# Loading the first x rows as four tiles instead of two halves, with per-tile transposes and a shorter warm-up, in a fused MLP forward and backward kernel

## The chip, the cores and the metric

The kernel runs on one core of one Trainium2 chip. The metric is device time in microseconds (us). All comparisons below are between runs in the fast state (the state in which nearly all executions agree); one profile that fell in a slow state is named where it occurs and is not used, and of two kernels that were run once only (e14 and e15), whose state cannot be judged, the profile is read and no time is compared. "Span" is the length of one execution in its trace; it is mostly about 1.8 us shorter than the reported time of the same run.

## The reference

`x` is 2048 x 640, `w1` 640 x 1536, `w2` 1536 x 640, all bfloat16. The reference computes the output and the three gradients.

```
h   = x @ w1
a   = silu(h)
out = a @ w2
# and, by jax.vjp with grad_out: grad x, grad w1, grad w2
```

## The kernel before

All x rows are worked on in four chunks of 512 rows. Every matmul of the first stage (`h = x @ w1`) needs x transposed, with the 640 columns on the partitions in five slices (`DT` = 5). For chunks 1 to 3 a DMA transpose does that. For the first chunk the kernel wants to begin early, so it loads plain x rows, transposes them on the tensor engine (PE), and copies the result from PSUM to `xT`. Some instructions, collected in `early`, are moved ahead of the barrier that every engine passes at entry.

```python
NWARM = 22                     # dummy matmuls that keep PE busy while data arrives
KM = 2                         # the first two slices of w1 come first
warm = cpool.tile([P, P], dt_in, name="warm")
early = [nc.vector.memset(warm[:], 1.0)]
for i in range(NWARM):
    early.append(nc.tensor.matmul(wp[:, 0:P], lhsT=warm[:], rhs=warm[:], start=True, stop=True))
# ... cut ...
def load_x_half(half):         # 256 rows, two neighbouring rows on each partition: 2,560 B runs
    lo = half * 2 * P
    return nc.sync.dma_start(
        out=x_two[:, half, :, :], in_=x2[lo:lo + 2 * P, :].rearrange("(p q) d -> p q d", q=2)
    )

def load_w1_rows(lo, hi):      # row blocks of w1, first 512 columns
    return nc.sync.dma_start(out=w1_nat[:, lo:hi, 0:FC], in_=w1_v[:, lo:hi, 0:FC])

early += [load_x_half(0), load_x_half(1), load_w1_rows(0, 1), load_w1_rows(1, KM)]
load_w1_rows(KM, DT)
start_before_entry_wait(nc, {i.ins.name for i in early})
for fc in range(1, NFC):
    load_w1(fc * FC, (fc + 1) * FC)
# ... cut ...
def pe_x_half(xT, half):
    lo = half * 2 * P
    for dt_ in range(DT):
        tp = ps_h.tile([P, 2, P], dt_in, name="tp", tag="hp")
        for q in range(2):
            nc.tensor.transpose(tp[:, q, :], x_two[:, half, q, dt_ * P:(dt_ + 1) * P], ident[:])
        copy = nc.scalar.copy if dt_ % 2 else nc.vector.tensor_copy
        copy(out=xT[:, dt_, lo:lo + 2 * P].rearrange("p (s q) -> p q s", q=2), in_=tp[:])
```

The first stage then starts with slices 0 and 1 of four output blocks (eight matmuls of 512 columns), and only the ninth matmul needs slices 2 to 4:

```python
def h_first(xT, aT, ghT):
    # ...
    for dt_ in range(KM):                    # eight matmuls: w1 row blocks 0 and 1
        for ft in range(FB):
            h_mm(hps[ft], ft, xT, dt_, dt_ + 1)
    for i in range(FT + LAG_G):
        if i < FT:
            if i < FB:
                h_mm(hps[i], i, xT, KM, DT)  # the ninth matmul and on: w1 row blocks 2 to 4
    # ... cut ...
```

Below, the first, second and third w1 load are `load_w1_rows(0, 1)`, `load_w1_rows(1, KM)` and `load_w1_rows(KM, DT)`, which bring row block 0, row block 1 and row blocks 2 to 4 (384 KB). They are the same loads in both kernels.

Of the kernel before, what the change touches and what calls it, by code (L numbers as in the profile page):

```python
# [42 lines left out]
def kernel(  # L43
# [11 lines left out]
    nc = tc.nc  # L55
    P = 128
    x2 = x.flatten_outer_dims()
# [5 lines left out]
    S, D = x2.shape  # L63
    F = w1.shape[1]
    ST, DT, FT = S // P, D // P, F // P
    SC = 512
    NCH = S // SC
    STC = SC // P
# [3 lines left out]
    LAG = 2  # L72
    LAG_G = 4
    KM = 2
    NWARM = 22
    dt_in = x.dtype

    dram = ctx.enter_context(tc.tile_pool(name="dram", bufs=1, space=bass.MemoryType.DRAM))
# [2 lines left out]
    ps_h = ctx.enter_context(tc.tile_pool(name="ps_h", bufs=8, space=bass.MemoryType.PSUM))  # L81
# [8 lines left out]
    x_nat = natpool.tile([P, ST, D], dt_in, name="x_nat")  # L90
# [3 lines left out]
    x_v = x2.rearrange("(st p) d -> p st d", p=P)  # L94
# [4 lines left out]
    def store_rows(c, pool):  # L99
        for scr, dst_v in ((oT_scr, out_v), (gxT_scr, gx_v)):  # L100
            o_sb = pool.tile([P, STC, D], dt_in, name="o_sb")
            nc.sync.dma_start_transpose(out=o_sb[:], in_=scr[:, c * SC:(c + 1) * SC])
            nc.sync.dma_start(out=dst_v[:, c * STC:(c + 1) * STC, :], in_=o_sb[:])
# [8 lines left out]
    with ExitStack() as mctx:  # L112
        cpool = mctx.enter_context(tc.tile_pool(name="cpool", bufs=1))
# [7 lines left out]
        early = [nc.vector.memset(warm[:], 1.0)]  # L121
        warm_a = cpool.tile([P, 1], FP32, name="warm_a")
        wp = ps_h.tile([P, SC], FP32, name="wp", tag="hp")
        for i in range(NWARM):
            early.append(nc.tensor.matmul(wp[:, 0:P], lhsT=warm[:], rhs=warm[:], start=True, stop=True))

        ident = cpool.tile([P, P], dt_in, name="ident")
# [7 lines left out]
        def load_xT(c):  # L135
            xT = xpool.tile([P, DT, SC], dt_in, name="xT")
            nc.sync.dma_start_transpose(out=xT[:], in_=x2[c * SC:(c + 1) * SC, :])
            return xT

        def load_goT(c):  # L140
            goT = xpool.tile([P, DT, SC], dt_in, name="goT")
            nc.sync.dma_start_transpose(out=goT[:], in_=go2[c * SC:(c + 1) * SC, :])
            return goT

        xT_next = xpool.tile([P, DT, SC], dt_in, name="xT")
        x_two = cpool.tile([P, 2, 2, D], dt_in, name="x_two")

        def load_w1(lo, hi):
            nc.sync.dma_start(out=w1_nat[:, :, lo:hi], in_=w1_v[:, :, lo:hi])

        def load_x_half(half):
            lo = half * 2 * P
            return nc.sync.dma_start(
                out=x_two[:, half, :, :], in_=x2[lo:lo + 2 * P, :].rearrange("(p q) d -> p q d", q=2)
            )

        def load_w1_rows(lo, hi):
            return nc.sync.dma_start(out=w1_nat[:, lo:hi, 0:FC], in_=w1_v[:, lo:hi, 0:FC])

        early += [load_x_half(0), load_x_half(1), load_w1_rows(0, 1), load_w1_rows(1, KM)]  # L160
        load_w1_rows(KM, DT)
        start_before_entry_wait(nc, {i.ins.name for i in early})
        for fc in range(1, NFC):
# [5 lines left out]
            nc.sync.dma_start_transpose(out=w2T[:, :, fc * FC:(fc + 1) * FC], in_=w2[fc * FC:(fc + 1) * FC, :])  # L169
        nc.sync.dma_start_transpose(out=w1T[:], in_=w1[:, :])  # L170

        def pe_x_half(xT, half):
            lo = half * 2 * P
            for dt_ in range(DT):
                tp = ps_h.tile([P, 2, P], dt_in, name="tp", tag="hp")
                for q in range(2):
                    nc.tensor.transpose(tp[:, q, :], x_two[:, half, q, dt_ * P:(dt_ + 1) * P], ident[:])  # L177
                copy = nc.scalar.copy if dt_ % 2 else nc.vector.tensor_copy
                copy(out=xT[:, dt_, lo:lo + 2 * P].rearrange("p (s q) -> p q s", q=2), in_=tp[:])  # L179

        pe_x_half(xT_next, 0)
        pe_x_half(xT_next, 1)

        def h_mm(hp, ft, xT, lo, hi):
            for dt_ in range(lo, hi):
# [20 lines left out]
        def h_group(ft, xT, aT, ghT):  # L206
            hp = ps_h.tile([P, SC], FP32, name="hp")
            h_mm(hp, ft, xT, 0, DT)
            silu_a(ft, hp, aT)
            silu_grad(ft, hp, aT, ghT)  # L210

        def h_first(xT, aT, ghT):
            hps = []
            for ft in range(FB):
                hps.append(ps_h.tile([P, SC], FP32, name="hp"))
            for dt_ in range(KM):
# [5 lines that stand above are left out]
                        h_mm(hps[i], i, xT, KM, DT)  # L222
                    else:
                        hps.append(ps_h.tile([P, SC], FP32, name="hp"))
                        h_mm(hps[i], i, xT, 0, DT)
                    silu_a(i, hps[i], aT)
                if i >= LAG_G:
                    silu_grad(i - LAG_G, hps[i - LAG_G], aT, ghT)

        def g_group(ft, goT, ghT):  # L230
            gp = ps_h.tile([P, SC], FP32, name="hp")
            for dt_ in range(DT):
                nc.tensor.matmul(  # L233
                    gp[:],
                    lhsT=w2T[:, dt_, ft * P:(ft + 1) * P],
                    rhs=goT[:, dt_, :],
                    start=(dt_ == 0),
                    stop=(dt_ == DT - 1),
                )
            nc.vector.scalar_tensor_tensor(  # L240
                out=ghT[:, ft, :], in0=ghT[:, ft, :], scalar=1.0, in1=gp[:], op0=ALU.add, op1=ALU.mult
            )

        def sd_phase(c, w_all, rhs_all, scr):
            oT = opool.tile([P, DT, SC], dt_in, name="oT")
            for dt_ in range(DT):
                op_ = ps_h.tile([P, SC], FP32, name="hp")
                for ft in range(FT):
                    nc.tensor.matmul(  # L249
                        op_[:],  # L250
                        lhsT=w_all[:, ft, dt_ * P:(dt_ + 1) * P],
                        rhs=rhs_all[:, ft, :],
                        start=(ft == 0),
                        stop=(ft == FT - 1),
                    )
                if dt_ % 2 == 0:
                    nc.scalar.activation(oT[:, dt_, :], op_[:], ACT.Copy)  # L257
                else:
                    nc.vector.tensor_copy(out=oT[:, dt_, :], in_=op_[:])  # L259
            nc.sync.dma_start(  # L260
                out=scr[:, c * SC:(c + 1) * SC].rearrange("(dt p) s -> p dt s", p=P), in_=oT[:]
            )

        for c in range(NCH):
            xT, goT = xT_next, goT_next
            aT = apool.tile([P, FT, SC], dt_in, name="aT")
            ghT = apool.tile([P, FT, SC], dt_in, name="ghT")

            if c + 1 < NCH:
                xT_next = load_xT(c + 1)  # L270
                goT_next = load_goT(c + 1)
            if c == 1:
                for j in range(0, ST, STC):
                    nc.sync.dma_start(out=go_nat[:, j:j + STC, :], in_=go_v[:, j:j + STC, :])
            if c == 2:
                for j in range(0, ST, STC):
                    nc.sync.dma_start(out=x_nat[:, j:j + STC, :], in_=x_v[:, j:j + STC, :])

            if c == 0:
                h_first(xT, aT, ghT)  # L280
                nc.sync.dma_start(
                    out=aT_scr[:, c * SC:(c + 1) * SC].rearrange("(ft p) s -> p ft s", p=P), in_=aT[:]
                )
                sd_phase(c, w2_nat, aT, oT_scr)
                for ft in range(FT):
                    g_group(ft, goT, ghT)
                nc.sync.dma_start(
                    out=ghT_scr[:, c * SC:(c + 1) * SC].rearrange("(ft p) s -> p ft s", p=P), in_=ghT[:]
                )
                sd_phase(c, w1T, ghT, gxT_scr)  # L290
                continue

            for i in range(FT + LAG):
                if i < FT:
                    h_group(i, xT, aT, ghT)
                if i >= LAG:
                    g_group(i - LAG, goT, ghT)

            store_rows(c - 1, opool)
            nc.sync.dma_start(  # L300
                out=aT_scr[:, c * SC:(c + 1) * SC].rearrange("(ft p) s -> p ft s", p=P), in_=aT[:]
            )
            nc.sync.dma_start(
                out=ghT_scr[:, c * SC:(c + 1) * SC].rearrange("(ft p) s -> p ft s", p=P), in_=ghT[:]
            )
            if c == NCH - 1:
                load_a_blk(0, w1pool, "w1a")

            sd_phase(c, w2_nat, aT, oT_scr)
            sd_phase(c, w1T, ghT, gxT_scr)  # L310

    with ExitStack() as fctx:
# [45 lines left out]
        for fc in range(NFC):  # L358
            gh_blk = gh_blks[fc]
            for dt_ in range(DT):  # L360
                if dt_ == DT // 2:
                    store_gw2(fc)
                if fc == NFC - 1 and dt_ == DT - 1:
                    for k, (lo, hi) in enumerate(((0, FC - P), (FC - P, FC))):
# [12 lines left out]
                        else:  # L377
                            nc.vector.tensor_copy(out=g1[:, lo:hi], in_=gp[:, lo:hi])  # L378
                        nc.sync.dma_start(
                            out=gw1_v[:, dt_, fc * FC + lo:fc * FC + hi], in_=g1[:, lo:hi]  # L380
# [48 lines left out]
```

## Time and profile before

| | before |
|---|---|
| median of the first three runs | 321.46 us (320.92 to 321.84) |
| span of the profiled run | 318.9 us |
| PE busy | 315.2 us, 99% of the span |
| first real matmul starts | 5.01 us |

The first fence is the head of the page, then the share of the chain of waits by engine. Columns of the first line: busy time, share of the span, number of instructions.

```profile
PE 315.2 (99%) x1498; PEld 145.4 (46%) x1498; DVE 102.2 (32%) x182; ACT 77.7 (24%) x142; POOL 0.7 (0%) x6
...
PE 98%; DMA 1%; DVE 1%; issue 0%; DVEq 0%; SPq 0%
...
L186 PE MATMUL hp<-xT,w_nat 128*128 128x512 bf16 x240 | 56.9, 379 | 0.2 <-DVE xT L179 0.2
```

PE is the bound. The `| 0.2` in the last line is all the idle time just before first-stage matmuls. So, apart from a tail of 2.9 us after the last matmul, only the head, before the first real matmul, can shrink. The next fence is the chain of waits of the kernel before in its first 22 us; columns are start, duration and what the chain went through.

```profile
0.09 2.94 DMA x_two<-in_x_dram
...
3.08 0.41 PE tp L177 x2
3.49 0.02 issue
3.51 1.46 DVE xT L179 x4
4.97 0.04 issue
5.01 13.11 PE hp L186 x60
```

Read it from top to bottom: the first half of x lands, two transposes, four VectorE copies back to back, then 60 matmuls without a gap. The timeline of PE alone in the first 12 us of the kernel before (start, duration, count, and in brackets what ended the idle time before) shows warm-up, transposes and first stage:

```profile
0.50 2.53 PE L125 MATMUL wp<-warm 128*128 128x128 bf16 x22 [0.50 <-DVE warm L121]
3.08 1.70 PE L177 MATMUL tp<-ident,x_two 128*128 128x128 bf16 x20
5.01 7.28 PE L186 MATMUL hp<-xT,w_nat 128*128 128x512 bf16 x33 [0.23 <-DVE xT L179]
```

The pitch, start to start, tells the clock. The start times in the trace give 0.107 us for a 128-column matmul up to about 3.6 us and 0.056 us after; from 5.01 us a 512-column matmul starts every 0.216 us. So the array went from half to full speed near 3.6 us. Finally, the landing times of w1's three row-block loads (issue to completion, minimum, median, maximum), and the traffic between 3.5 and 5.5 us, where the last two columns are the share of the 16 DMA engines in use and GB/s:

```profile
DMA to landing us min/median/max: 3.3/3.7/4.2
```

```profile
core 0: us, PE busy (x) PEld busy (x) DVE busy (x) ACT busy (x) POOL busy (x), PEclk, DMA share, GB/s
3.50:5.50 2.00, 1.76 (x21) 1.23 (x20) 1.99 (x6) 1.51 (x4) 0.00 (x0) 1.00 0.97 312
```

The third w1 load, issued at 2.04 us, takes the 4.2 us and has landed at 6.22 us. The ninth matmul, which needs it, starts at 6.73 us (the ninth start time in the trace; 5.01 + 8 x 0.216 us gives the same). The DMA engines are full, 0.97 of the 16 in use from 3.5 to 5.5 us.

### The profile page before, as it was taken

Reading aid. Unit: us, or ns where it says so; the run is one execution under the profiler, and the core shown is the slowest. Engines: PE = TensorE matmul, PEld = TensorE weight load, DVE = VectorE, ACT = ScalarE, POOL = GpSimd, SP = SyncE. Lnnn points to the kernel's source line nnn. Section 1 sums busy time; section 2 is a strip of 40 time slices with the busy share of each in tenths; the row PEclk is TensorE's granted clock in tenths of the full one; section 3 lists DMA queues with packets and bytes.
Section 4 is the critical chain, followed back from the end, with each engine's and each line's share of the span. In section 5 each row is a group of like instructions: output and inputs, shape, how many; then the busy total and the mean of one; then the engine's idle time right before and its main releaser. Section 6 shows DMA issues by size and latency. Waiting matters only on the chain.

```text
span 318.9 us, 3570 instructions
## 1 busy us (share of the span) xinstructions
PE 315.2 (99%) x1498; PEld 145.4 (46%) x1498; DVE 102.2 (32%) x182; ACT 77.7 (24%) x142; POOL 0.7 (0%) x6
## 2 busy tenths in 40 slices
PE   9999999999999999999999999999999999999996
PEld 6444444444444444444444444444444444444443
DVE  2871641477410187700157741000001100001001
ACT  4951000644201354311065410111000001001100
POOL 0000000000000000000000000000000000000000
DMA  8999999998999866382643089719999998995011
GB/s 274 319 173 221 250 243 277 334 289 264 290 288 305 199 200 166 109 286 82 166 128 119 2 279 264 200 45 285 272 207 270 262 249 288 239 293 194 34 48 34
DMA packets 147311, 67.33 MB, mean 211 GB/s; under 512 B 112608, under 2 KB 147040, under 8 KB 147296
## 3 DMA queue, kind: packets, MB, share of 16 engines
q1 hardware_dynamic: 147296, 67.12, 81.5%
q8 instruction: 11, 0.18, 0.2%
q14 instruction: 4, 0.03, 0.0%
HBM read 9.83 MB, written 28.97 MB: 122 GB/s over the span
## 4 chain that ended last, share of the span: by engine, by line
PE 98%; DMA 1%; DVE 1%; issue 0%; DVEq 0%; SPq 0%
PE hp L249 32%; PE hp L186 16%; PE hp L337 16%; PE hp L233 16%; PE hp L385 15%; PE hp L367 1%; DMA x_two<-in_x_dram 1%; DVE xT L179 0%; PE tp L177 0%; DVE g L378 0%; DVEq L378 0%; SPq L413 0%
## 5 line engine op out<-in xcount | busy, mean ns | idle before, releaser
L186 PE MATMUL hp<-xT,w_nat 128*128 128x512 bf16 x240 | 56.9, 379 | 0.2 <-DVE xT L179 0.2
L233 PE MATMUL hp<-goT,w2T 128*128 128x512 bf16 x240 | 56.9, 379 | 0.0
L249 PE MATMUL hp<-aT,w_nat 128*128 128x512 bf16 x240 | 52.5, 379 | 0.0
L249 PE MATMUL hp<-ghT,w1T 128*128 128x512 bf16 x240 | 52.5, 379 | 0.0
L337 PE MATMUL hp<-a_blk,go_nat 128*128 128x512 bf16 x240 | 52.0, 379 | 0.0
L385 PE MATMUL hp<-gh_blk,x_nat 128*128 128x512 bf16 x224 | 48.5, 379 | 0.0
L257 ACT ACTIVATE oT<-hp 128x512 bf16<-128x512 f32 x24 | 14.3, 597 | 109.8 <-PE hp L249 109.8
L195 ACT ACTIVATE aT<-hp 128x512 bf16<-128x512 f32 x48 | 29.9, 625 | 32.8 <-PE hp L186 32.8
L186 PEld LDWEIGHTS <-w_nat 128*128 128x128 bf16 x240 | 23.5, 98 | 28.4 <-issue 0.4
L233 PEld LDWEIGHTS <-w2T 128*128 128x128 bf16 x240 | 23.5, 98 | 28.3
L337 PEld LDWEIGHTS <-go_nat 128*128 128x128 bf16 x240 | 23.5, 98 | 28.3
L249 PEld LDWEIGHTS <-w1T 128*128 128x128 bf16 x240 | 23.5, 98 | 28.3
L249 PEld LDWEIGHTS <-w_nat 128*128 128x128 bf16 x240 | 23.4, 98 | 28.3
L259 DVE CAST oT<-hp 128x512 bf16<-128x512 f32 x16 | 11.1, 692 | 77.0 <-PE hp L249 77.0
L240 DVE SCALAR_TENSOR_TENSOR ghT<-ghT,hp 128x512 bf16<-128x512 bf16 x48 | 32.5, 681 | 7.3 <-PE hp L233 7.3
L385 PEld LDWEIGHTS <-x_nat 128*128 128x128 bf16 x224 | 21.9, 98 | 26.4
L202 DVE SCALAR_TENSOR_TENSOR ghT<-aT,v 128x512 bf16<-128x512 bf16 x48 | 32.7, 686 | 0.5
L201 DVE TENSOR_SCALAR v<-t 128x512 bf16<-128x512 f32 x48 | 20.2, 425 | 30.1 <-ACT t L199 30.1
L199 ACT ACTIVATE t<-hp 128x512 f32<-128x512 f32 x48 | 29.8, 625 | 0.0
L396 DVE CAST g<-hp 128x512 bf16<-128x512 f32 x7 | 4.8, 691 | 47.1 <-PE hp L385 27.6
L347 DVE CAST g2T<-hp 128x512 bf16<-128x512 f32 x7 | 4.8, 692 | 46.1 <-PE hp L337 46.1
L345 ACT ACTIVATE g2T<-hp 128x512 bf16<-128x512 f32 x8 | 4.8, 597 | 47.0 <-PE hp L337 47.0
(20 smaller groups left out, 25.2 us busy)
## 6 DMA issues: line engine op xcount, KB each, us to landing
aT_scr<-aT SPq DMA_DIRECT2D x4, 1536.0 KB, 7.1
ghT_scr<-ghT SPq DMA_DIRECT2D x4, 1536.0 KB, 8.0
out_dram<-o_sb SPq DMA_DIRECT2D x8, 640.0 KB, 3.6
oT_scr<-oT SPq DMA_DIRECT2D x4, 640.0 KB, 3.6
go_nat<-in_grad_out_dram SPq DMA_DIRECT2D x4, 640.0 KB, 6.6
x_nat<-in_x_dram SPq DMA_DIRECT2D x4, 640.0 KB, 5.4
gxT_scr<-oT SPq DMA_DIRECT2D x4, 640.0 KB, 4.7
w_nat<-in_w_dram SPq DMA_DIRECT2D x1, 1920.0 KB, 13.7
```

Of the source, the lines that this page charges most:

```text
L186: nc.tensor.matmul(hp[:], lhsT=w1_nat[:, dt_, ft * P:(ft + 1) * P], rhs=xT[:, dt_, :], start=(dt_ == 0), stop=(dt_ == DT - 1),)
L195: nc.scalar.activation(aT[:, ft, :], hp[:], ACT.Silu)
L199: nc.scalar.activation(t[:], hp[:], ACT.Tanh, scale=0.5)
L201: nc.vector.tensor_scalar(out=v[:], in0=t[:], scalar1=-0.5, scalar2=0.5, op0=ALU.mult, op1=ALU.add)
L202: nc.vector.scalar_tensor_tensor(out=ghT[:, ft, :], in0=aT[:, ft, :], scalar=1.0, in1=v[:], op0=ALU.subtract, op1=ALU.mult)
L233: nc.tensor.matmul(gp[:], lhsT=w2T[:, dt_, ft * P:(ft + 1) * P], rhs=goT[:, dt_, :], start=(dt_ == 0), stop=(dt_ == DT - 1),)
L240: nc.vector.scalar_tensor_tensor(out=ghT[:, ft, :], in0=ghT[:, ft, :], scalar=1.0, in1=gp[:], op0=ALU.add, op1=ALU.mult)
L249: nc.tensor.matmul(op_[:], lhsT=w_all[:, ft, dt_ * P:(dt_ + 1) * P], rhs=rhs_all[:, ft, :], start=(ft == 0), stop=(ft == FT - 1),)
L257: nc.scalar.activation(oT[:, dt_, :], op_[:], ACT.Copy)
L259: nc.vector.tensor_copy(out=oT[:, dt_, :], in_=op_[:])
L337: nc.tensor.matmul(gp[:], lhsT=go_nat[:, st, dt_ * P:(dt_ + 1) * P], rhs=a_blk[:, st, :], start=(st == 0), stop=(st == ST - 1),)
L385: nc.tensor.matmul(gp[:], lhsT=x_nat[:, st, dt_ * P:(dt_ + 1) * P], rhs=gh_blk[:, st, :], start=(st == 0), stop=(st == ST - 1),)
```

## The change

The intent is to start on x sooner: four loads of 128 rows, each transposed as it lands into two PSUM tiles, so that two copies per tile suffice (VectorE slices 0 and 1, ScalarE slices 2 to 4). The tiles go straight to `x_nat`, which saves one later load. As the first tile is expected sooner, the warm-up is cut.

```diff
-    NWARM = 22
+    NWARM = 16
...
-        def load_x_half(half):
-            lo = half * 2 * P
-            return nc.sync.dma_start(
-                out=x_two[:, half, :, :], in_=x2[lo:lo + 2 * P, :].rearrange("(p q) d -> p q d", q=2)
-            )
+        def load_x_tile(st):
+            return nc.sync.dma_start(out=x_nat[:, st, :], in_=x_v[:, st, :])
...
-        early += [load_x_half(0), load_x_half(1), load_w1_rows(0, 1), load_w1_rows(1, KM)]
+        early += [load_x_tile(st) for st in range(STC)]
+        load_w1_rows(0, 1)
+        load_w1_rows(1, KM)
         load_w1_rows(KM, DT)
...
-        def pe_x_half(xT, half):
... (body cut, see above)
+        def pe_x_tile(xT, st):
+            for copy, lo, hi in ((nc.vector.tensor_copy, 0, KM), (nc.scalar.copy, KM, DT)):
+                tp = ps_h.tile([P, hi - lo, P], dt_in, name="tp", tag="hp")
+                for dt_ in range(lo, hi):
+                    nc.tensor.transpose(tp[:, dt_ - lo, :], x_nat[:, st, dt_ * P:(dt_ + 1) * P], ident[:])
+                copy(out=xT[:, lo:hi, st * P:(st + 1) * P], in_=tp[:])
...
-                for j in range(0, ST, STC):
+                for j in range(STC, ST, STC):
                     nc.sync.dma_start(out=x_nat[:, j:j + STC, :], in_=x_v[:, j:j + STC, :])
```

More of the change, by code (lines that the diff above doesn't have):

```diff
@@ L145 @@
         xT_next = xpool.tile([P, DT, SC], dt_in, name="xT")
-        x_two = cpool.tile([P, 2, 2, D], dt_in, name="x_two")
         def load_w1(lo, hi):
             nc.sync.dma_start(out=w1_nat[:, :, lo:hi], in_=w1_v[:, :, lo:hi])
-        def load_x_half(half):
-            lo = half * 2 * P
-            return nc.sync.dma_start(
-                out=x_two[:, half, :, :], in_=x2[lo:lo + 2 * P, :].rearrange("(p q) d -> p q d", q=2)
-            )
+        def load_x_tile(st):
+            return nc.sync.dma_start(out=x_nat[:, st, :], in_=x_v[:, st, :])
         def load_w1_rows(lo, hi):
             return nc.sync.dma_start(out=w1_nat[:, lo:hi, 0:FC], in_=w1_v[:, lo:hi, 0:FC])
-        early += [load_x_half(0), load_x_half(1), load_w1_rows(0, 1), load_w1_rows(1, KM)]
+        early += [load_x_tile(st) for st in range(STC)]
+        load_w1_rows(0, 1)
+        load_w1_rows(1, KM)
         load_w1_rows(KM, DT)
@@ L170 @@
         nc.sync.dma_start_transpose(out=w1T[:], in_=w1[:, :])
-        def pe_x_half(xT, half):
-            lo = half * 2 * P
-            for dt_ in range(DT):
-                tp = ps_h.tile([P, 2, P], dt_in, name="tp", tag="hp")
-                for q in range(2):
-                    nc.tensor.transpose(tp[:, q, :], x_two[:, half, q, dt_ * P:(dt_ + 1) * P], ident[:])
-                copy = nc.scalar.copy if dt_ % 2 else nc.vector.tensor_copy
-                copy(out=xT[:, dt_, lo:lo + 2 * P].rearrange("p (s q) -> p q s", q=2), in_=tp[:])
-        pe_x_half(xT_next, 0)
-        pe_x_half(xT_next, 1)
+        def pe_x_tile(xT, st):
[4 more added lines that the diff above has]
+                copy(out=xT[:, lo:hi, st * P:(st + 1) * P], in_=tp[:])
+        for st in range(STC):
+            pe_x_tile(xT_next, st)
         def h_mm(hp, ft, xT, lo, hi):
```

## The prediction

> **What bounds the kernel.** The tensor engine. The page gives PE 315.2 us busy of a 318.9 us span (99%); the chain of waits is PE for 98%. Parts:
> - Head, to 5.01 us: DMA of x_two (0.09 to 3.03), transposes (3.08), four VectorE copies (3.51 to 4.97), first real matmul at 5.01.
> - Body, to about 316: matmuls without a gap. The first 60 take 12.95 us to the next group's start, 216 ns each, as all later ones, so the clock was full by 5.01. The groups show 0.2 us of PE idle in L186 and 0.0 in the others.
> - Tail: a small copy and the last store.
>
> The diff touches the head and one load in the third chunk (x_nat, 70 to 84 us), which PE needs only at 264 us: removing it is worth 0. Only tenths of a microsecond of the head can change.
>
> **What the change does to the head.**
> 1. Arrival. Half 0 was waited for until 3.03, half 1 until 4.04; the windows show 340 to 380 GB/s once the queue runs. The same 640 KB now come as four loads. Estimate from those bytes: landing near 2.55, 3.05, 3.5 and 4.0. Rows shrink from 2,560 to 1,280 B: [...]w1's 1,024 B rows move at about 320 GB/s here, so I expect at most 0.1 us of loss.
> 2. After the last arrival. Before: 4.04 to 5.01 = 0.97 us, as VectorE still copied half 0. Now two transposes (estimate 0.28 us, from the 219 ns matmul) and one 128x256 copy (0.45 us) give about 0.77 us: first matmul near 4.8. ScalarE's slices (estimate 0.55 us) are needed eight matmuls later. Gain about 0.2 us.
> 3. w1. Its first row blocks were issued at 1.00 and 1.5; now behind four x loads and the entry barrier, near 2.0 and 2.5 (0.41 us an issue). They queued behind x anyway, so should land nearly as before (row 0 near 4.4). Margins are thin: w1's second column block, issued at 2.48, lands 6.6 us later at 9.08 and is needed at 5.01 + 20 x 0.216 = 9.33. Starting 0.2 us earlier uses that margin up; a DMA bubble of 0.1 to 0.2 us turns part of the gain into a wait in L182.
> 4. Warm-up, 22 to 16 matmuls: at 115 ns each it ends near 2.34, not 3.03, just before the first tile lands. [...]the trace has full speed by 4.04 after a start at 0.50. Tiles every 0.5 us keep the array mostly busy, so I expect the full clock by the first real matmul. If not, 8 to 16 matmuls at half speed cost 1.5 to 3 us.
>
> **Sum.** -0.2 (copies) +0.1 (w1, DMA) = about -0.1 us. Predicted 321.3 us, range 320.7 to 322.1; the runs before spread 0.9 us. Faster by over 2%: 0.01; within 2%: 0.98; slower: 0.01.
>
> **What would show it.** Right: first L182 matmul at 4.7 to 5.0, then no idle and 216 ns pitch; last x tile landing near 4.0; span 318.6 to 319.1. Wrong in step 2: the last VectorE x copy begins over 0.4 us after the last tile lands. Wrong in step 3: idle before L182, released by w1's DMA. Wrong in step 4: pitch near 430 ns in L182.
>
> **What would make it wrong.** w1's first rows landing after 4.9; a throttled clock[...].

What is cut are grounds that no trace or run of this case shows: one of two for the 0.1 us allowed in step 1, which now rests on the 1,024 B rows of w1 alone (before: 295 GB/s from 5 to 6 us, 328 from 6 to 7); one of two for the full clock by the first real matmul in step 4, which now rests on the one trace of the kernel before (full near 3.6 us); and a last risk, about semaphores, that no run met. The 0.55 us of ScalarE's copy was the author's estimate (measured 0.480 us), and it is not in the sum.

## The result

| | before | changed |
|---|---|---|
| median, six runs each | 321.56 us (320.92 to 321.84) | 323.06 us (322.86 to 323.36) |
| ratio of mean fast runs | | 1.0051, 95% interval 1.0038 to 1.0064 |
| span of the profiled run | 318.9 us | 321.2 us |

The change makes the kernel 0.5% slower, clear of noise, and outside the predicted range of 320.7 to 322.1 us. A ratio here and below is the mean time of one kernel's fast runs over that of the other's of the same rounds, so it is not quite the ratio of the medians quoted beside it.

The page of the changed kernel, same lines:

```profile
PE 316.9 (99%) x1492; PEld 145.7 (45%) x1492; DVE 101.4 (32%) x180; ACT 78.1 (24%) x142; POOL 0.7 (0%) x6
...
PE 96%; DMA 2%; SPq 0%; DVE 0%; issue 0%; DVEq 0%
...
L182 PE MATMUL hp<-xT,w_nat 128*128 128x512 bf16 x240 | 58.4, 386 | 0.3 <-DMA w_nat<-in_w_dram 0.3
```

The chain of waits of its first 22 us:

```profile
2.90 6.01 DMA w_nat<-in_w_dram
8.91 0.05 issue
8.96 11.40 PE hp L182 x52
```

The chain no longer goes through x. It goes through the third w1 load, issued at 2.90 and landing at 8.91 us, and then through 52 matmuls, not 60: the first eight had run before and do not count. The PE timeline of its first 12 us:

```profile
0.50 1.89 PE L125 MATMUL wp<-warm 128*128 128x128 bf16 x16 [0.50 <-DVE warm L121]
2.42 1.25 PE L174 MATMUL tp<-ident,x_nat 128*128 128x128 bf16 x10
4.13 1.25 PE L174 MATMUL tp<-ident,x_nat 128*128 128x128 bf16 x10 [0.47 <-DMA x_nat<-in_x_dram]
5.44 3.26 PE L182 MATMUL hp<-xT,w_nat 128*128 128x512 bf16 x8
8.96 3.41 PE L182 MATMUL hp<-xT,w_nat 128*128 128x512 bf16 x15 [0.25 <-DMA w_nat<-in_w_dram]
```

Two things went wrong at once here. The eight matmuls from 5.44 us take 3.26 us, about 0.43 us each, which is half speed, where 0.216 us each was expected; the trace's clock record turns to full at 8.25 us. And behind them PE waits 0.25 us for w1. Landing times of the three w1 row-block loads, and the traffic from 3.5 to 5.5 us:

```profile
DMA to landing us min/median/max: 2.9/3.3/6.0
```

```profile
3.50:5.50 2.00, 1.47 (x13) 1.13 (x12) 0.76 (x3) 1.19 (x4) 0.00 (x0) 1.00 0.75 202
```

The traffic falls from 312 to 202 GB/s while the DMA engines are busy only 0.75 of the time. A warning on reading: the column before the last two, the granted clock, says 1.00 here although the pitch shows half speed. The clock record of this trace begins only with its first transition, at 8.25 us. Read a clock from the pitch of the matmuls.

From here on PE works without a gap, so the start of the ninth matmul sets the end. It moved from 6.73 to 8.96 us, by 2.23 us, and the spans differ by 2.3 us. The profiled run before was a quick one; the medians differ by 1.5 us, and a possible reason for this scatter, which was not shown, is given below.

### The profile page after: what moved, and what is told of

It reads as the page before. It is cut to its first block, busy times and chain, and to the rows that moved or that the text cites. A ratio compares the mean times of both kernels' runs of the same rounds, so it can differ in the third digit from the quotient of the medians.

```text
span 321.2 us, 3558 instructions
## 1 busy us (share of the span) xinstructions
PE 316.9 (99%) x1492; PEld 145.7 (45%) x1492; DVE 101.4 (32%) x180; ACT 78.1 (24%) x142; POOL 0.7 (0%) x6
## 4 chain that ended last, share of the span: by engine, by line
PE 96%; DMA 2%; SPq 0%; DVE 0%; issue 0%; DVEq 0%
PE hp L245 32%; PE hp L229 16%; PE hp L333 16%; PE hp L182 16%; PE hp L381 15%; DMA w_nat<-in_w_dram 2%; PE hp L363 1%; SPq L154 0%; DVE g L374 0%; DVEq L374 0%
## 5 line engine op out<-in xcount | busy, mean ns | idle before, releaser
L182 PE MATMUL hp<-xT,w_nat 128*128 128x512 bf16 x240 | 58.4, 386 | 0.3 <-DMA w_nat<-in_w_dram 0.3
```

The costliest lines, as they stand in the source:

```text
L182: nc.tensor.matmul(hp[:], lhsT=w1_nat[:, dt_, ft * P:(ft + 1) * P], rhs=xT[:, dt_, :], start=(dt_ == 0), stop=(dt_ == DT - 1),)
```

## The experiments

Two theories to begin with. **Clock**: the shorter warm-up and the gaps between tiles leave the array at half speed until 8.25 us. **Loads**: four x loads push the w1 loads back and the third w1 load comes late. A third, **both-overlap**: each holds the same ninth matmul to about 8.9 us, so that undoing one alone gives little back.

All runs named below gave correct results. The summary comes first. "Third w1" is the landing of the load that brings w1's row block 2 in the profiled run; "full clock" is when the array goes to full speed in that run, from the clock record or, where marked p, from the pitch; GB/s is from 3.5 to 5.5 us. The medians of the kernel before are those of the same chip.

| run | median us | before us | ratio, 95% interval | third w1 us | full clock us | GB/s |
|---|---|---|---|---|---|---|
| before (first profile) | 321.56 | | | 6.22 | 3.6 p | 312 |
| changed (first profile) | 323.06 | 321.56 | 1.0051 (1.0038 to 1.0064) | 8.91 | 8.25 | 202 |
| e1: changed, 22 warm-ups | 322.56 | 321.08 | 1.0042 (1.0028 to 1.0055) | 8.05 | 6.16 | 227 |
| e2: changed, two x loads, w1 early | 322.27 | 321.08 | 1.0040 (1.0024 to 1.0055) | 6.98 | 7.29 | 279 |
| e3: e1 and e2 together | 321.53 | 321.08 | 1.0020 (0.9999 to 1.0041) | 7.00 | 6.06 | 275 |
| e4: before, 16 warm-ups | 322.56 | 321.08 | 1.0038 (1.0021 to 1.0055) | 6.36 | 8.88 | 292 |
| e5: before, four x loads | 322.34 | 321.33 | 1.0037 (1.0018 to 1.0055) | 7.19 | 3.30 | 200 |
| e6: changed, PE filled | 322.57 | 321.33 | 1.0034 (1.0018 to 1.0051) | 7.16 | 4.99 | 200 |
| e7: changed, 22 warm-ups, w1 by ScalarE | 325.90 | 321.33 | 1.0145 (1.0126 to 1.0164) | 7.89 | 4.81 | 250 |
| e8: before, w1 by ScalarE | 323.01 | 321.33 | 1.0064 (1.0042 to 1.0086) | 9.07 | 6.2 p | 301 |
| e9: two x loads, w1 late | 321.71 | 321.42 | 1.0011 (0.9986 to 1.0036) | 7.59 | 6.24 | 205 |
| e10: before, 16 wide warm-ups | 321.41 | 321.42 | 0.9988 (0.9970 to 1.0006) | (slow profile) | | |
| e11: before, 26 warm-ups | 321.30 | 321.42 | 0.9998 (0.9974 to 1.0023) | 6.42 | 6.08 | 285 |
| e12: changed again | 322.60 | 321.42 | 1.0032 (1.0012 to 1.0053) | 8.67 | 3.90 | 214 |
| e13: one w1 load | 324.18 | 321.01 | 1.0127 (1.0079 to 1.0175) | 7.07 | (no record) | 282 |
| e14: e9 again, one run | 322.52 | 321.01 | one run | 7.08 | 4.01 | 223 |
| e15: changed, third time, one run | 323.34 | 321.01 | one run | 8.10 | 9.9 p | 214 |

### The change undone in halves: e1 to e4

e1, in the changed kernel:

```diff
-    NWARM = 16
+    NWARM = 22
```

> The changed kernel with 22 warm-up matmuls again, nothing else. Clock theory (the shorter warm-up let the tensor clock stay at half speed until 8.25 us, and that is the whole loss): full clock by the first L182 matmul, pitch 216 ns, time back to 321.6 +- 0.4 us. Load theory (four x loads push the w1 rows behind the entry barrier, they land at 8.9 instead of 6.2 us, and that is the whole loss): about 323.0 us as the changed kernel, with PE waiting over 1 us for w1's third row block. Both-overlap theory (either alone holds the ninth L182 matmul to about 8.9 us): 322.7 to 323.0 us, clock full early, and the wait for w1 grows to about 1.5 us.

Measured: 322.56 us, ratio 1.0042; the interval overlaps that of the changed kernel, so nothing was clearly won. In the profile the clock is full at 6.16 us, in the middle of the eight matmuls, and the time that saves turns into a longer wait (0.55 us, where the both-overlap theory had about 1.5):

```profile
5.63 1.92 PE L182 MATMUL hp<-xT,w_nat 128*128 128x512 bf16 x7
8.10 6.22 PE L182 MATMUL hp<-xT,w_nat 128*128 128x512 bf16 x28 [0.55 <-DMA w_nat<-in_w_dram]
```

(This is the PE timeline of e1; one matmul record of the eight is missing in this trace.) The clock theory as the whole cause is out.

e2, in the changed kernel:

```diff
-        def load_x_tile(st):
-            return nc.sync.dma_start(out=x_nat[:, st, :], in_=x_v[:, st, :])
+        def load_x_pair(st):
+            return nc.sync.dma_start(out=x_nat[:, st:st + 2, :], in_=x_v[:, st:st + 2, :])
-        early += [load_x_tile(st) for st in range(STC)]
-        load_w1_rows(0, 1)
-        load_w1_rows(1, KM)
+        early += [load_x_pair(0), load_x_pair(2), load_w1_rows(0, 1), load_w1_rows(1, KM)]
```

> The changed kernel with the x rows in two loads of two tiles each and the first two w1 row blocks issued before the entry barrier again, still 16 warm-up matmuls and tile-wise transposes. Clock theory: no gain, about 323 us, eight or more L182 matmuls at 427 ns. Load theory: w1's third row block lands near 6.2 us and the time goes back to 321.6 +- 0.4 us. Both-overlap theory: the wait for w1 vanishes, the cold matmuls stay: 322.5 to 323.0 us.

Measured: 322.27 us, ratio 1.0040, with no wait for w1 named in the PE timeline but full clock only at 7.29 us. Loads as the whole cause are out too; the both-overlap theory had 322.5 to 323.0, slightly high.

e3 has both edits.

> Both edits together. All three theories expect the time of the kernel before or slightly less, 321.2 to 321.7 us: full clock by the first L182 matmul, which starts at 4.7 to 5.1 us, and no wait for w1. If it stays near 323 us, the tile-wise transposes and copies themselves cost something and all three are wrong.

Measured: 321.53 us, ratio 1.0020 with an interval that just reaches 1. So the two undone together give back most of it, and the tile-wise transposes and copies, which are still in this kernel, neither cost nor win anything that shows. The time is as expected, the head is not: in the profile the first real matmul starts at 5.60 us, not by 5.1, and the clock is full only at 6.06 us.

e4, in the kernel before:

```diff
-    NWARM = 22
+    NWARM = 16
```

> The kernel before with 16 warm-up matmuls, nothing else. Clock theory: slower by about 1.5 us (323.0), with half speed in the first L182 matmuls up to about 8 us. Load theory: 321.6 us, no change. Both-overlap theory: slower by 1.0 to 1.7 us, since the cold matmuls alone cost 8 x 0.21 us.[...]

Measured: 322.56 us, ratio 1.0038. One constant costs 1.5 us by the medians in a kernel whose loads are untouched. PE timeline of e4:

```profile
0.51 1.89 PE L125 MATMUL wp<-warm 128*128 128x128 bf16 x16 [0.51 <-DVE warm L121]
3.13 2.31 PE L177 MATMUL tp<-ident,x_two 128*128 128x128 bf16 x20 [0.73 <-DMA x_two<-in_x_dram]
5.25 9.08 PE L186 MATMUL hp<-xT,w_nat 128*128 128x512 bf16 x32
```

The gap ahead of the transposes has grown to about 0.9 us (the last warm-up starts at 2.09 and lasts 0.107, the transposes begin at 3.13), and the clock is full at 8.88 us only. One of its six runs took 321.25 us, which may be a run that found the clock open early (that run has no trace).

### The other halves: e5 and e6

e5 puts the loads of the change into the kernel before, with 22 warm-ups and its own transposes:

```diff
-                out=x_two[:, half, :, :], in_=x2[lo:lo + 2 * P, :].rearrange("(p q) d -> p q d", q=2)
+                out=x_two[:, half, q, :], in_=x2[lo:lo + 2 * P, :].rearrange("(p q) d -> p q d", q=2)[:, q, :]
...
-        early += [load_x_half(0), load_x_half(1), load_w1_rows(0, 1), load_w1_rows(1, KM)]
+        early += [load_x_quarter(half, q) for half in range(2) for q in range(2)]
+        load_w1_rows(0, 1)
+        load_w1_rows(1, KM)
```

> The kernel before (22 warm-ups, its own transposes and copies) with its x rows in four loads of 160 KB and all w1 row blocks issued after the entry barrier, so the loads alone are as in the change. Load theory: w1's third row block lands at 8.0 to 9.0 us instead of 6.2 and PE waits for it over 0.7 us; time 1.0 to 1.6 us over the kernel before of this chip. Clock theory: no loss, within 0.3 us of the kernel before. Both-overlap theory: as the load theory.

Measured: 322.34 us, ratio 1.0037, as the load theory had it. The profile itself is milder than expected: the third w1 load lands at 7.19, not past 8.0 us, and the three waits for w1 in it add up to 1.6 us of the weight loads' time, none over 0.6 us. The clock was full at 3.30 us here, so the loads cost time without its help. The profiled run was the shortest of the six by span (319.5 us against a median of 320.5).

e6 keeps the loads of the change, has 22 warm-ups and fills PE's gaps with matmuls that nobody reads:

```diff
+        def fill(n):
+            fp = ps_h.tile([P, SC], FP32, name="fp", tag="hp")
+            for i in range(n):
+                nc.tensor.matmul(fp[:, 0:P], lhsT=warm[:], rhs=warm[:], start=True, stop=True)
         for st in range(STC):
             pe_x_tile(xT_next, st)
+            if st == 1:
+                fill(5)
+            if st == STC - 1:
+                fill(3)
```

> The changed kernel with 22 warm-ups, five filler matmuls after the second tile and three after the fourth, so that the tensor engine is never idle before the first L182 matmul; loads untouched. Clock theory: [...]time within 0.4 us of the kernel before. Load theory and both-overlap theory: at most 0.5 us better than the changed kernel (ratio 1.003 to 1.005), and a wait of 0.3 to 1.7 us for w1's third row block, which lands after 8 us whatever the clock does.

Measured: 322.57 us, ratio 1.0034: keeping PE busy does not rescue the loads. But the profile shows no wait for w1 before the first-stage matmuls, against what was written; it landed at 7.16 us in this run, which again was the shortest of its six by span (319.7 against a median of 320.7). So the long wait is not shown for e6, only the time.

### The changed kernel again: e12 and e15

> The changed kernel again, on this chip, for a second profile of it: ratio 1.004 to 1.006, w1's third row block landing between 7.1 and 9.0 us, traffic dip from 3.5 to 5.5 us.[...]

> The changed kernel a third time, for the clock and the landing: third row block between 7.1 and 9.0 us; [...]whichever of the two is later holds PE.

These two are, with the first profile, the clearest evidence, as they show one unchanged program in three clock conditions. (The ratio of e12, 1.0032, is a little under what was expected; the landing and the dip are as expected.) In e12 the clock was full at 3.90 us. PE timeline of e12:

```profile
3.95 0.45 PE L174 MATMUL tp<-ident,x_nat 128*128 128x128 bf16 x5 [0.35 <-DMA x_nat<-in_x_dram]
4.91 0.45 PE L174 MATMUL tp<-ident,x_nat 128*128 128x128 bf16 x5 [0.51 <-DMA x_nat<-in_x_dram]
5.58 1.89 PE L182 MATMUL hp<-xT,w_nat 128*128 128x512 bf16 x8 [0.22 <-DVE xT L175]
8.71 3.63 PE L182 MATMUL hp<-xT,w_nat 128*128 128x512 bf16 x16 [1.25 <-DMA w_nat<-in_w_dram]
```

From the chain of waits of e12, the third w1 load:

```profile
2.89 5.78 DMA w_nat<-in_w_dram
```

Now the eight matmuls take 1.89 us, not 3.26, and the wait behind them is 1.25 us, not 0.25. The ninth matmul starts only 0.25 us sooner, about as much as the load landed sooner (0.24 us); the rest of what the clock gave went into the wait. In e15 the clock was not full until about 9.9 us, while the third w1 load landed at 8.10 us: no matmul of the first stage waits for w1, and they run at half speed past the ninth. From the PE timeline of e15, and the landing times of its w1 row-block loads (the third, issued at 2.90 us, takes the 5.2 us):

```profile
5.47 6.84 PE L182 MATMUL hp<-xT,w_nat 128*128 128x512 bf16 x21
DMA to landing us min/median/max: 3.0/3.5/5.2
```

| profile | full clock | third w1 landed | ninth matmul starts | span less 318.9 |
|---|---|---|---|---|
| before | 3.6 | 6.22 | 6.73 | 0 |
| changed | 8.25 | 8.91 | 8.96 | 2.3 |
| e12, changed | 3.90 | 8.67 | 8.71 | 2.0 |
| e15, changed | 9.9 | 8.10 | 8.83 | 2.7 |

The sums close. The ninth matmul is later by 2.23, 1.98 and 2.10 us; in e15 the ninth and the two after it also run wholly or partly at half speed, 0.21 + 0.21 + 0.09 = 0.5 us more, which makes 2.6 of the 2.7.

### When does the clock open? e10 and e11

e10, in the kernel before: 16 warm-up matmuls of 176 columns instead of 22 of 128, so that they end together.

```diff
-    NWARM = 22
+    NWARM = 16
-        warm = cpool.tile([P, P], dt_in, name="warm")
+        warm = cpool.tile([P, 176], dt_in, name="warm")
-            early.append(nc.tensor.matmul(wp[:, 0:P], lhsT=warm[:], rhs=warm[:], start=True, stop=True))
+            early.append(nc.tensor.matmul(wp[:, 0:176], lhsT=warm[:, 0:P], rhs=warm[:], start=True, stop=True))
```

> The kernel before with 16 warm-up matmuls of 176 columns instead of 22 of 128, so that they end at the same 2.85 us. If the time that PE is busy before the tiles come decides the clock: same time as the kernel before (within 0.3 us)[...]. If the number of warm-up matmuls decides: 1.2 to 1.5 us slower as with 16 of 128 columns.

Measured: 321.41 us against 321.42, ratio 0.9988 (0.9970 to 1.0006). As e4, with 16 warm-ups of 128 columns, was at 1.0038, the time follows the busy time of the warm-ups and not their count; the clock itself is not shown for e10. Its profiled run (granted clock 0.95, 334.51 us) is not read.

e11, in the kernel before:

```diff
-    NWARM = 22
+    NWARM = 26
```

> The kernel before with 26 warm-ups, which end at 3.3 us, after the first half of x has landed, so PE has no gap there. Candidate for a better version. If [...]the gap of 0.26 us before was already tolerated: same time within 0.3 us, with the same spread of 0.7 to 1.3 us between runs. If the gap delayed the clock in some runs, the slow ones vanish: median 0.2 us lower and a spread under 0.5 us.

Measured: 321.30 us, ratio 0.9998 (0.9974 to 1.0023). The kernel before already had enough, and its runs still scatter (320.87 to 321.82 us, and one of 323.28).

The profiles show a scatter in the opening itself. In those with 22 or more warm-ups the clock opened anywhere from 3.3 to 6.2 us (e13, whose opening is not recorded, is left out); with 16 of 128 columns, in five profiles, at 3.90, 7.29, 8.25, 8.88 and about 9.9 us. That is one value before 4 us, and nothing from there to 7.29. (That the scatter of the unprofiled times comes from it is argued, not shown, as only profiled runs have start times.)

What sets the moment was not shown. By the start times, with 0.107 us of work for each 128-column matmul at half speed, PE was idle in the first profile of the changed kernel for 0.24 us after the warm-ups and for 0.67 us before the third tile, together 0.9 us by 4.13 us, and the array stayed at half speed until 8.25 us. In the kernel before it was idle for 0.26 us after the warm-ups, and the clock opened near 3.6 us.

### Why does w1 land late? e7, e8, e9, e13, e14

e7 takes the changed kernel with 22 warm-ups and lets ScalarE issue the three w1 loads, before the barrier; e8 does the same in the kernel before.

```diff
-            return nc.sync.dma_start(out=w1_nat[:, lo:hi, 0:FC], in_=w1_v[:, lo:hi, 0:FC])
+            return nc.scalar.dma_start(out=w1_nat[:, lo:hi, 0:FC], in_=w1_v[:, lo:hi, 0:FC])
```

> The changed kernel with 22 warm-ups and the three w1 row loads issued by ScalarE's queue before the entry barrier, at 0.1 to 1.4 us, beside the four x loads; sizes and bytes untouched. If the late issue (2.0 to 2.9 us behind the x loads) is what delays w1: the third row block lands by 6.5 us, x tiles land up to 0.4 us later, time within 0.4 us of the kernel before. If small loads or 1,280 B rows as such make the DMA engines slow: it lands after 7.5 us still and the time stays 1 us or more above. Clock theory makes no difference between this and the run with 22 warm-ups alone (ratio 1.004).

> A candidate for a better version: the kernel before with its three w1 row loads on ScalarE's queue before the entry barrier. If the start of the queue is limited by one issuer, w1's third row block lands before 5.8 us and the time falls by 0 to 0.5 us (321.1 to 320.7); if x and w1 only share the same bandwidth, x's second half lands about 0.4 us later and the time rises by up to 0.4 us.

Both failed as kernels: e7 took 325.90 us (ratio 1.0145) and e8 323.01 us (1.0064). In e7 the last x tile is waited for until 7.38 us, PE timeline of e7:

```profile
2.83 1.28 PE L172 MATMUL tp<-ident,x_nat 128*128 128x128 bf16 x10
4.97 0.45 PE L172 MATMUL tp<-ident,x_nat 128*128 128x128 bf16 x5 [0.86 <-DMA x_nat<-in_x_dram]
7.38 0.45 PE L172 MATMUL tp<-ident,x_nat 128*128 128x128 bf16 x5 [1.96 <-DMA x_nat<-in_x_dram]
```

and after this wait of 1.96 us the clock record shows half speed again, from 8.22 to 11.64 us (full from 4.81). In e8 the third w1 load, issued at 1.12 us, takes 7.96 us, and PE waits for it until 9.12 us. So in these two runs, with two queues, a load came late that is needed early: the last x tile in e7 (PE waited for it until 7.38 us, in e1, without the move, until 4.85) and the third w1 load in e8 (landed at 9.07 us, before at 6.22). In e7 the third w1 load, issued at 1.12 us, landed at 7.89 us, which by the text would speak for the small loads; but e7 did not answer the question it was made for, as it took the late issue away but also the single queue.

e9 is cleaner. It is e1 with two large x loads, followed by two loads of 2 KB that only fill two issue slots:

```diff
-        def load_x_tile(st):
-            return nc.sync.dma_start(out=x_nat[:, st, :], in_=x_v[:, st, :])
+        def load_x_pair(st):
+            return nc.sync.dma_start(out=x_nat[:, st:st + 2, :], in_=x_v[:, st:st + 2, :])
+        def load_pad(k):
+            pad = cpool.tile([16, 64], dt_in, name=f"pad{k}")
+            return nc.sync.dma_start(out=pad[:], in_=x2[0:16, 0:64])
-        early += [load_x_tile(st) for st in range(STC)]
+        early += [load_x_pair(0), load_x_pair(2), load_pad(0), load_pad(1)]
```

> The changed kernel with 22 warm-ups and x in two large loads, followed by two tiny loads (2 KB each) that only take up issue slots, so that w1's row loads are issued at about the times of the changed kernel (2.0 to 2.9 us) though x is not split in four. If the late issue delays w1: the traffic from 3.5 to 5.5 us dips to about 200 GB/s on average as in all runs with four loads (before: 312), w1's third row block lands at 7.2 us or later, median span 1.0 to 1.4 us over the kernel before. If the small x loads are the cause: traffic about 275 GB/s and landing at 7.0 us as with two loads alone, span 0.3 us over the kernel before.

> The two-loads-late kernel again for a second landing. Late issue alone: dip again, third row block at 7.1 to 9.0 us. Four small loads as a further cause: below 7.7 us again, while kernels with four loads reach 8.0 to 8.9 us in three of five profiles.

Measured: the traffic dips as in the runs with four loads, 205 GB/s (223 in e14), where e3 with the same two large loads and early w1 has 275. The windows of e9 and of e3:

```profile
3.50:5.50 2.00, 2.00 (x18) 1.66 (x17) 1.16 (x4) 1.43 (x3) 0.00 (x0) 1.00 0.86 205
```

```profile
3.50:5.50 2.00, 2.00 (x20) 1.87 (x18) 1.12 (x4) 1.42 (x3) 0.00 (x0) 1.00 1.01 275
```

So the dip comes with the late issue of w1: in e9 most of x has landed by about 4 us (12 of the 16 completion events of the second x load by 3.90 us), and the traffic is at 140 to 190 GB/s from 4.0 to 5.25 us. But the third w1 load lands at 7.59 and 7.08 us, not past 8, and the time is only 1.0011 of that of the kernel before, where the late issue was expected to cost 1.0 to 1.4 us. Late issue is a part, not the whole. By the times it is the smaller part: e9 does not differ from e3, where w1 is issued early (1.0020), while e1, with w1 late and x in four loads, is at 1.0042 (e9 ran on another chip than these two, and the intervals of e9 and e1 just overlap, so this is likely and not shown). (e14's 322.52 us comes from another wait, 1.07 us for w1's second column block, which landed at 10.92 us in that run.)

e13 keeps four x loads and takes the late issue away, with one w1 load for all five row blocks:

```diff
-        load_w1_rows(0, 1)
-        load_w1_rows(1, KM)
-        load_w1_rows(KM, DT)
+        early.append(load_w1_rows(0, DT))
```

> The changed kernel with 22 warm-ups and w1's five row blocks in one 640 KB load issued before the entry barrier, at about 1.9 us instead of 2.0 to 2.9 us in three loads; four x loads kept. If the late issue causes the dip in traffic: the mean from 3.5 to 5.5 us is above 270 GB/s and all rows have landed by 6.8 us (PE's first L182 matmul then waits for them, so the time need not fall: span 319.8 to 320.8 us). If four small x loads slow the engines: the dip to about 200 GB/s stays and they land at 7.1 us or later.

Measured: 282 GB/s; the dip after 4 us is gone, which again says late issue, though a short one to about 175 GB/s remains from 3.5 to 4.0 us. But all rows had landed at 7.07 us, not by 6.8, and since the first matmul waits for all of them the kernel takes 324.18 us.

The windows of e13:

```profile
3.50:5.50 2.00, 1.84 (x16) 1.31 (x14) 0.95 (x4) 1.55 (x4) 0.00 (x0) 1.00 0.90 282
```

Together: with the loads of the kernel before the third w1 load landed at 6.22 to 6.42 us (three profiles); with two loads of 1,280-byte rows and early issue at 6.98 and 7.00; with these and late issue at 7.08 and 7.59; with four loads and late issue at 7.16, 7.19, 8.05, 8.10, 8.67 and 8.91. The trace shows 16 completion events for each load. In the first profile of the changed kernel 14 of the 16 of this load had come by 6.93 us; the last two came at 8.32 and 8.91. Such a lag, of one event in e15 to six in e12, stands in four of the six profiles with four loads and late issue (changed, e1, e12, e15). It is there before w1: in the same four the last x tile landed at 4.5 to 4.9 us, in the other two (e5 and e6) at 4.0 us. Those two ran on another chip than e1, e12 and e15, but each was also the shortest run of its kernel. What makes the last events lag stays open.

## Why the prediction was wrong, point by point

- **What bounds the kernel, and that only the head can change**: right. PE stays without a gap after the ninth matmul, and the removed load in the third chunk changed nothing visible.
- **Step 1, arrival**: estimated 2.55, 3.05, 3.5 and 4.0 us; by the completion events 2.37, 2.85, 4.09 and 4.55 us. The last two came 0.55 to 0.6 us late; of the third tile 14 of the 16 completion events had come by 3.46 us, and the last came at 4.09. For the row size the prediction allowed 0.1 us. The runs do not settle it. With four loads of 1,280 B rows all x had landed by 3.99 us (e5) and 4.03 us (e6), as in the kernel before (4.00 us), so rows of this size need not be slower; in five other profiles it took until 4.5 to 4.9 us. In the two-load kernels with 1,280 B rows the third w1 load landed at 7.0 us, with 2,560 B rows at 6.2 to 6.4. (Number and order of the loads are the same in both; with the 1,280 B rows the third w1 load was issued 0.13 us later, at 2.17 against 2.04 us.)
- **Step 2, copies**: the copy was even quicker than estimated, 0.292 instead of 0.45 us for 128x256, and still the first real matmul came at 5.44, not 4.8 us. Of these 0.64 us, 0.55 are the late last tile (step 1). From its landing to the first matmul it took 0.89 us where 0.77 was estimated. The term that was mis-sized here is the transposes: the ten of the last two tiles took 1.25 us at half speed, from 4.13 us, so that the last VectorE copy began at 5.10 us, 0.55 us after the tile landed (the prediction's own sign was 0.4). In e12, with the clock open, it took 0.72 us from landing to first matmul.
- **Step 3, "should land nearly as before", failed.** Row block 0 landed at 4.90, not 4.4; the third w1 load at 8.91 instead of 6.22 us. The prediction worked out margins for w1's second column block but not for the third w1 load, which had only 6.73 - 6.22 = 0.5 us. It assumed that a load queued behind x does not care when it is issued. The runs showed a dip from 312 to 202 GB/s once x was through, and e9, e14 and e13 tie that dip to the issue at 2.0 to 2.9 us. But the late issue alone accounts for only part of the delay (7.08 and 7.59 us in e14 and e9), and the rest, which comes with the four loads, has no shown cause. Split and late issue together cost ratio 1.0037 in the kernel before (e5).
- **Step 4, "I expect the full clock by the first real matmul", failed.** The array was at half speed until 8.25 us (0.43 us a matmul, not 0.216). The tiles did not come every 0.5 us: the third landed 1.24 us after the second, and with the gap after the warm-ups PE was idle for about 0.9 us by 4.13 us. That this idle time is what kept the clock down was not shown. Sixteen warm-ups alone cost ratio 1.0038 in the kernel before (e4). The price that the prediction named for this case, 1.5 to 3 us, was right; the judgement that it was unlikely was wrong, since it took one trace's early opening (3.6 us) as the kernel's, where the opening differs from run to run (8.25, 3.90 and about 9.9 us in three profiles of the changed kernel).
- **The sum** failed a third way: the prediction treated the two risks as separate terms. They are a maximum, not a sum. Either alone can hold the ninth matmul to about 8.7 us (8.71 in e12 by the load, 8.65 in e4 by the clock), though it was less in other profiles (8.10 in e1, 8.19 in e2, 7.23 in e5). That is why e1 and e2 gave so little and why the loss is 1.5 us by the medians and not 3.

No version tried beats the kernel before: 26 warm-ups and 16 wide ones equal it, and e3, the changed transposes with the old loads' issue order and warm-up, is 1.0020 of it at an interval that touches 1.

## What to carry to other kernels

When several inputs must arrive before an engine can run on, write down for each the time it lands and the time it is needed, and look at the smallest margin; in the changed kernel a load issued 0.86 us later, behind more and smaller loads, landed 1.9 to 2.7 us later. Size a warm-up by its busy time (here 16 of 128 columns instead of 22 cost ratio 1.0038, and 16 of 176 columns nothing that shows, 0.9988), and judge its effect over several runs, because one trace shows one opening of the clock (3.90, 8.25 and about 9.9 us in three profiles of one kernel). If undoing one suspect gives nothing back, undo both before acquitting either.
